# A fixed place in each step for the products that give a row maximum, the difference product last, and five summed tiles in place of four on TensorE

## The chip, the cores and the metric

The kernel runs on one core of a Trainium2 chip. The metric is the device time in microseconds (us) of one execution; lower is better. The numbers of before are the median of three timed runs and one further execution under the hardware profiler, from which all rows of the trace come.

## The reference

Three stages follow each other. Only the first is touched by the change: attention over 2 batches of 8 heads, with 1152 keys of 64 dimensions, and queries that are averaged in twos, so that 576 are left.

```python
q_pool = q.reshape(B, H, S // factor, factor, D).mean(axis=3)
scores = scale * np.matmul(q_pool, k.transpose(0, 1, 3, 2))
scores = scores - np.max(scores, axis=-1, keepdims=True)
attn = np.exp(scores)
attn = attn / (np.sum(attn, axis=-1, keepdims=True) + 1e-09)
return np.matmul(attn, v).astype(np.float32)
```

Its output, 1152 rows of 512, goes through a mixture of experts (8 experts, one per row) and then a dense block with the weights `w_in` and `w_out`.

## The kernel before

The attention works on 8 pairs of heads, p = 0 to 7. A pair has 9 steps, t = 0 to 8, one for each 128 keys. The engines' orders are written out by hand: what the Python loop emits first stands first in the queue of its engine, and each engine works its queue strictly in that order.

**A step** of pair p does three things on TensorE. `scores` makes the transposed scores of 128 keys against all 576 queries of both heads (8 matrix products, L287 to L296), and ScalarE turns them into exponentials, the tile `Pt[p, t]`. `pv` multiplies the exponentials of the step before with the values (L304). And a few products for the row maxima of the next pair, p + 1, are put between.

**The maxima.** The query rows of a pair are cut into 9 units, four of 128 queries for each head and one mixed one. For each unit the 1152 keys are handled in three chunks of 384. Chunk c = 0 is reduced by VectorE (L103). Chunk c = 1 isn't the keys but their difference, `KD` (tile `kx`, made by GpSimd: keys 384 to 767 minus keys 768 to 1151); ScalarE takes the positive part of the product into the buffer `wd` (tile name `wd<-mx` at L91). Chunk c = 2 is added to that and reduced by VectorE (L240). So 27 products per pair, each into one of three PSUM banks called `mx`, which are taken in turn. The same three banks serve `sum_log` (step 2, L344, emptied by ScalarE into `sm`), `sum_tr` (step 3, L351, emptied by `sum_rec` on VectorE in step 4), the output's transposes (L401, steps 5 and 6) and `max_rows` (step 8, L268), which turns the finished maxima into rows for the next pair's scores.

**The denominators.** The exponentials of all keys must be summed. VectorE adds tiles into `St` (`add_tile`, one addition of 128 x 1152), and `psums` sums a tile over its keys with a matrix of ones, on TensorE (L324).

**The end of a pair.** In step 0 of the following pair the last `pv` and `psums` come, and `post_evac` empties the accumulators: ScalarE copies them (`wd<-pv`, `sm<-pv`), then VectorE adds into `sm` (`sm<-pv,sm`). The accumulators are one set, so the first `pv` of the new pair, in step 1, waits for this addition.

**Decoding.** Between all this, a packed weight matrix for the last stage is decoded in 23 blocks. A block is loaded by SyncE into one of two buffers `wraw`; ScalarE takes the absolute value of one half (`dm<-wraw`), GpSimd clamps it, and VectorE does two halves of bit work: part 0 reads `wraw` (`ds<-wraw` twice), part 1 writes the weights (`dm<-dm`, `wd<-dm,ds`). A load waits until part 0 of the block two before is done, since that frees its buffer. In pairs 0 to 6 four or five such halves are done in a pair; pair 7 has no maxima to prepare and does 15 of them (`DEC_L`).

**The order in a step** is spelt by a string: `0` is `scores`, `m` a place for one waiting task and one product, `r` `max_rows`, `p` `pv` with `psums`, `s` and `t` the two sum pieces. Tasks that find no place are emitted at the end of the step.

Of the kernel before, what the change touches and what calls it, by code (L numbers as in the profile page):

```python
# [29 lines left out]
NPAIR = B * H // 2  # L30
KT = S // P
# [53 lines left out]
def kernel(ctx, tc, cst, qt, kt, v, wgo, w1, w2, wio, out):  # L85
# [71 lines left out]
    Pt, pvt = {}, {}  # L157
# [84 lines left out]
    def ahead(units):  # L242
        n = len(units)
        seq_ = [(units[0], 0), (units[0], 1)]
        for i in range(n):
            if i + 1 < n:
                seq_ += [(units[i + 1], 1)]
            seq_ += [(units[i], 2)]
            if i + 1 < n:
                seq_ += [(units[i + 1], 0)]  # L250
        return [(*u, c) for u, c in seq_]

    chunks = ahead([(h, j) for h in range(2) for j in range(4)] + [(0, 4)])

    mfin = {}

# [43 lines left out]
    def pv(p, t, f):  # L300
        if t == 0 and f == 0:
            pvt[p] = pvp.tile([P, 2, 512], F32, name="pv")
        for h in range(2):
            mm(pvt[p][64 * h:64 * h + 64, f, :HQ], lhsT=vt[p][:, t, h, :], rhs=Pt[p, t][:, h, f * HQ:(f + 1) * HQ], start=t == 0, stop=t == KT - 1, skip_group_check=True)  # L304


    adds = {2: True, 3: False, 5: True, 6: False, 8: True}
    whole = {3: (0,), 6: (0,), 8: (0, 1)}
    St = {}

    def add_tile(p, t, new):
# [4 lines left out]
    def psums(p, t):  # L316


        for src in [(St[p], Pt[p, t])[i] for i in whole.get(t, ())]:
            for f in range(2):  # L320
                for h in range(2):
                    for a in range(2):
                        q_, t0 = 64 * h + 32 * a, 256 * a + 160 * f
                        mm(pvt[p][q_:q_ + 32, f, HQ:HQ + 160], lhsT=e2[:, h], rhs=src[:, h, t0:t0 + 160], start=False, stop=src is Pt.get((p, KT - 1)), skip_group_check=True)  # L324
# [13 lines left out]
    def sum_log(p):  # L338

        b, hp = divmod(p, 4)  # L340
        ps = mxp.tile([P, 512], F32, name="mx")
        for a in range(2):
            qs_ = slice(256 * a, 256 * a + 320)
            mm(ps[32 * a:32 * a + 32, :320], lhsT=wbd[:, hp], rhs=xut[p][:, qs_], start=True, stop=True)  # L344
        act(sm[:64, 64 * b:64 * b + 320], ps[:64, :320])

    def sum_tr(p):
        ps = mxp.tile([P, 512], F32, name="mx")
        slt[p] = ps[:, :384].rearrange("p (w c) -> p w c", w=3)
        for w in range(3):  # L350
            T.transpose(slt[p][:, w], sm[:, w * P:(w + 1) * P], ident)  # L351
# [215 lines left out]

    for g in range(-9, 9 * NPAIR):
        p, t = divmod(g, 9)
        if t == 0:  # L570
            todo = list(chunks) if p + 1 < NPAIR else []
        tasks = list(sched.get(g, ()))
        if p >= 0 and t in adds:
            tasks += [lambda: None] * (2 - len(tasks))
            tasks.insert(2, lambda p=p, t=t: add_tile(p, t, adds[t]))
        if p >= 0:
            n = DEC_L[t] if p == NPAIR - 1 else (t in (0, 1, 2, 8)) + (p % 2 and t == 3)
            tasks += [lambda: (raw_ahead(ap, DEC_A), decode_step(ap, DEC_A))] * n
            if t in ABS_T or p == NPAIR - 1:
                tasks.append(lambda: (raw_ahead(ap, DEC_A), decode_abs(ap)))  # L580

        slot = [0]

        def mxc(todo=todo):
            if tasks:
                tasks.pop(0)()
            if todo:
                max_chunk(p + 1, *todo.pop(0))
            slot[0] += 1

        prev = divmod(g - 1, 9)
        seq = "0mmrpsmmt" if p == NPAIR - 1 or t in (2, 3, 4, 8) else "0mmrpsmt"
        if g < 0:
            seq = "mmmm"
        assert not (t == 8 and todo), (p, len(todo))
        for ch in seq:
            if ch == "0":
                if p >= 0:
                    scores(p, t)
            elif ch == "m":  # L600
                mxc()
            elif ch == "s":
                if p > 0 and t == T_S:
                    sum_log(p - 1)
            elif ch == "t":
                if p > 0 and t == T_T:
                    sum_tr(p - 1)
            elif ch == "e":
                mxc([])
            elif ch == "r":  # L610
                if t == 8 and 0 <= p < NPAIR - 1:
                    max_rows(p + 1)
            elif ch in "pfg" and prev[0] >= 0:
                if ch in "pf":
                    pv(*prev, 0)
                if ch in "pg":
                    pv(*prev, 1)
                    psums(*prev)
                    if prev[1] == KT - 1:
                        post_evac(prev[0])  # L620
        for f in tasks:
            f()
        if p > 0 and t in (T_X - 1, T_X):
            x_tr(p - 1, t - T_X + 1)
        if g == -1:
            warm(6)
        if g == -1:
            max_rows(0)
            warm(2)
# [766 lines left out]
```

## Time and profile before

| | |
|---|---|
| median of 3 runs | 691.23 us (690.6 to 692.02) |
| profiled execution, its own time | 691.73 us |
| its span, first to last instruction | 689.9 us |
| outside the span | 1.83 us |
| mean granted TensorE clock | 0.981 of full speed |
| TensorE matmul busy | 638.6 us (93%) |
| VectorE busy | 510.7 us (74%) |
| ScalarE busy | 398.4 us (58%) |
| attention, steps of pairs 0 to 7 | from 22 us to 292 us of the span |

Read it like this: the busy share of TensorE comes from matrix products that are pipelined, with modelled ends, so it overstates the work; what counts is the distance from one start to the next. The start of a pair is where the first `scores` product (L287) of its step 0 starts: 22.26, 54.53, 88.96, 122.36, 156.48, 190.57, 225.30 and 257.73 us.

### The profile page before, as it was taken

What the parts mean: (1) busy time and instruction counts of PE and PEld (TensorE: products, weight loads), DVE (VectorE), ACT (ScalarE), POOL (GpSimd) and SP (SyncE); (2) the same over time, 40 slices, a digit from 0 to 9 for tenths busy, and PEclk for the clock granted to TensorE, in tenths of its full rate; (3) what the DMA queues carried; (4) which work ended last, traced back from release to release, by engine and by line L of the source; (5) the groups of instructions that cost most, each with busy time, mean ns of one, the idle gap of its engine ahead of it and who ended that gap; (6) DMA issues with size and microseconds to landing.
All of it is one profiled execution on the core that took longest, in us unless ns stands there. A gap on an engine that the chain in (4) does not pass through costs nothing. (4 is left out here: it accounts for less than half of the span.)

```text
span 689.9 us, 11179 instructions
## 1 busy us (share of the span) xinstructions
PE 638.6 (93%) x4079; PEld 495.4 (72%) x4079; DVE 510.7 (74%) x1028; ACT 398.4 (58%) x825; POOL 210.4 (31%) x178
## 2 busy tenths in 40 slices
PE   4899999999999998859979999988899999999997
PEld 3666666666666665529866977757788999999995
DVE  5777878787878888756653988314999977897775
ACT  7877676767676765425244538324665554555543
POOL 7531504142223114334121524202222232233322
PEclk9999999999999999979989999999999999999999
DMA  7673645453524204249479878561000020001001
GB/s 267 210 214 86 173 116 145 130 150 118 132 82 137 96 1 142 81 129 351 169 294 320 311 249 324 209 246 47 0 1 1 0 93 2 0 1 47 1 0 47
DMA packets 26641, 88.32 MB, mean 128 GB/s; under 512 B 2886, under 2 KB 7631, under 8 KB 22482
## 3 DMA queue, kind: packets, MB, share of 16 engines
q1 hardware_dynamic: 21264, 73.23, 30.2%
q0 software_dynamic: 3568, 8.79, 5.7%
q10 hardware_dynamic: 1746, 5.51, 2.3%
q8 instruction: 34, 0.56, 0.3%
q14 instruction: 29, 0.24, 0.1%
HBM read 79.65 MB, written 8.39 MB: 128 GB/s over the span
## 5 line engine op out<-in xcount | busy, mean ns | idle before, releaser
L91 ACT ACTIVATE pt<-sc 128x320 f32<-128x320 f32 (+1 forms) x216 | 94.6, 489 | 20.5 <-PE sc L289 18.0
L100 POOL TENSOR_SCALAR u<-u 128x384 f32<-128x384 f32 x48 | 59.8, 1247 | 152.5 <-ACT u L91 120.4
L304 PE MATMUL pv<-pt,vt 128*64 128x288 f32 x576 | 86.5, 423 | 0.6 <-DVE sm L94 0.5
L100 POOL TENSOR_SCALAR dm<-dm 128x512 f32<-128x512 f32 x23 | 51.6, 2242 | 83.5 <-ACT dm L91 76.1
L865 PE MATMUL zps<-yh,wh 128*128 128x384 f32 x188 | 64.4, 343 | 1.7 <-DVE n L97 1.7
L867 PE MATMUL zps<-yl,wh 128*128 128x384 f32 x188 | 63.5, 338 | 0.0
L866 PE MATMUL zps<-yh,wd 128*128 128x384 f32 x180 | 61.1, 340 | 0.0
L1305 PE MATMUL ops<-wh,gl 128*128 128x512 f32 x144 | 57.8, 404 | 3.0 <-DVE gl L94 2.4
L304 PEld LDWEIGHTS pv<-pt,vt 128*64 128x64 f32 x576 | 35.4, 137 | 32.0 <-issue 15.1
L1305 PE MATMUL ops<-wh,gh 128*128 128x512 f32 x144 | 56.8, 394 | 0.2 <-ACT gh L91 0.2
L1305 PE MATMUL ops<-wd,gh 128*128 128x512 f32 x135 | 53.1, 393 | 0.0
L226 PE MATMUL mx<-at,qs 128*128 128x384 f32 x120 | 40.5, 381 | 11.7 <-ACT at L91 6.7
L103 DVE TENSOR_REDUCE Mp<-mx 128x1 f32<-128x384 f32 x72 | 39.7, 551 | 8.1 <-PE mx L226 7.1
L91 ACT ACTIVATE wd<-mx 128x384 f32<-128x384 f32 x63 | 30.9, 493 | 25.4 <-PE mx L226 17.1
L240 DVE CUSTOM_DVE_ANT_0 wd<-mx,wd 128x384 f32<-128x384 f32 x63 | 34.7, 551 | 14.1 <-PE mx L230 7.3
L91 ACT ACTIVATE l<-n,two 128x384 f32<-128x384 f32 x48 | 29.5, 614 | 25.0 <-DVE n L97 25.0
L91 ACT ACTIVATE u<-zps 128x384 f32<-128x384 f32 x48 | 23.2, 483 | 32.8 <-PE zps L867 30.1
L97 DVE SCALAR_TENSOR_TENSOR l<-n,r 128x384 f32<-128x384 f32 x48 | 26.6, 554 | 19.8 <-ACT r L91 19.8
L865 PEld LDWEIGHTS zps<-yh,wh 128*128 128x128 f32 x188 | 35.6, 190 | 3.7 <-ACT r L91 2.0
L226 PEld LDWEIGHTS mx<-at,qs 128*128 128x128 f32 x120 | 22.2, 197 | 21.0 <-ACT at L91 6.9
L1305 PEld LDWEIGHTS ops<-wh,gl 128*128 128x128 f32 x144 | 27.0, 188 | 13.9 <-DVE gl L94 7.0
L91 ACT ACTIVATE gh<-n 128x384 fp32r<-128x384 f32 x48 | 24.8, 517 | 20.7 <-DVE n L97 20.2
(293 smaller groups left out, 1742.2 us busy)
## 6 DMA issues: line engine op xcount, KB each, us to landing
wt<-in_w SPq DMA_DIRECT2D x32, 1024.0 KB, 6.2
wraw<-in_wio SPq DMA_DIRECT2D x23, 512.0 KB, 4.5
kd<-in_kt SPq DMA_DIRECT2D x16, 576.0 KB, 3.8
vt<-in_v SPq DMA_DIRECT2D x8, 576.0 KB, 6.6
wraw<-in_wio ACTq DMA_DIRECT2D x9, 512.0 KB, 6.1
tq<-in_qt SPq DMA_DIRECT2D x12, 288.0 KB, 4.9
tq<-in_qt POOLq DMA_DIRECT2D x12, 288.0 KB, 4.3
pt<-in_qt SPq DMA_DIRECT2D x4, 576.0 KB, 5.8
```

The lines of the kernel that those rows point to most:

```text
L91: A.activation(out=out, in_=in_, func=func, **kw)
L97: V.scalar_tensor_tensor(out=out, in0=a, scalar=s, in1=b, op0=op0, op1=op1)
L100: eng.tensor_scalar(out=out, in0=a, scalar1=s1, scalar2=s2, op0=op0, op1=op1)
L103: V.tensor_reduce(out=out, in_=in_, axis=AX.X, op=op)
L226: mm(ps, lhsT=QS[p, h][:, j * P:(j + 1) * P], rhs=keys(h), start=True, stop=True)
L240: V.tensor_tensor_reduce(out=r_, in0=ps, in1=r_, scale=1.0, scalar=-3.0e38, op0=ALU.add, op1=ALU.max, accum_out=Mp[p % 2][:, h, j, 1:2])
L304: mm(pvt[p][64 * h:64 * h + 64, f, :HQ], lhsT=vt[p][:, t, h, :], rhs=Pt[p, t][:, h, f * HQ:(f + 1) * HQ], start=t == 0, stop=t == KT - 1, ...
L865: mm(out_, lhsT=a, rhs=c, start=first, stop=False)
L866: mm(out_, lhsT=b_, rhs=c, start=False, stop=False)
L867: mm(out_, lhsT=a, rhs=d, start=False, stop=last_)
L1305: mm(opt[b_, j], lhsT=(g_, g_, gl_)[i], rhs=(wo, wl_, wo)[i], start=f == 0 and i == 0, stop=f == NF - 1 and i == 2)
```

## The change

The string is gone, and two tables say which products belong to which step: `EARLY[t]` before `pv`, `LATE_[t]` after it. A unit's products c = 0 and c = 2 now stand before `pv`, and the next unit's c = 1 (the difference) after it, in the same step. In step 2 there are six products, three on either side; the first c = 1 of a pair is made already in step 8 of the pair before. The addition of step 8 is left out; `psums` sums five tiles in place of four: `St`, `St` and `Pt[p, 6]`, `Pt[p, 7]` and `Pt[p, 8]`. The decoding half of step 2 moves to step 3, the additional one of odd pairs from step 3 to step 8. Tasks are emitted before `pv` only with a product or while more than three are waiting (in step 8: all).

```diff
-    chunks = ahead([(h, j) for h in range(2) for j in range(4)] + [(0, 4)])
+    units = [(h, j) for h in range(2) for j in range(4)] + [(0, 4)]
+    chunks = ahead(units)
+    EARLY = [[(0, 0), (0, 2)], [(1, 0), (1, 2)], [(2, 0), (2, 2), (3, 1)]] + [[(i, 0), (i, 2)] for i in range(4, 9)] + [[]]
+    LATE_ = [[(1, 1)], [(2, 1)], [(3, 0), (3, 2), (4, 1)]] + [[(i, 1)] for i in range(5, 9)] + [[], [(0, 1)]]
...
-    adds = {2: True, 3: False, 5: True, 6: False, 8: True}
-    whole = {3: (0,), 6: (0,), 8: (0, 1)}
+    adds = {2: True, 3: False, 5: True, 6: False}
+    whole = {3: lambda p: (St[p],), 6: lambda p: (St[p], Pt[p, 6]), 8: lambda p: (Pt[p, 7], Pt[p, 8])}
...
-        for src in [(St[p], Pt[p, t])[i] for i in whole.get(t, ())]:
+        for src in whole[t](p) if t in whole else ():
...
-            n = DEC_L[t] if p == NPAIR - 1 else (t in (0, 1, 2, 8)) + (p % 2 and t == 3)
+            n = DEC_L[t] if p == NPAIR - 1 else (t in (0, 1, 3, 8)) + (p % 2 and t == 8)
...
-        seq = "0mmrpsmmt" if p == NPAIR - 1 or t in (2, 3, 4, 8) else "0mmrpsmt"
...
+            scores(p, t)
+            while todo or len(tasks) > (0 if t == 8 else 3):
+                mxc()
+            todo = late
+            if t == 8 and p < NPAIR - 1:
+                max_rows(p + 1)
+            if prev[0] >= 0:
+                for f in range(2):
+                    pv(*prev, f)
+                psums(*prev)
+                if prev[1] == KT - 1:
+                    post_evac(prev[0])
+            if p > 0 and t == T_S:
+                sum_log(p - 1)
+            while todo:
+                mxc()
+            if p > 0 and t == T_T:
+                sum_tr(p - 1)
```

TensorE in step 2 of pair 4, from the products before `pv` to the next step's first score product (before, then changed; `kx` is the difference, `at` the keys). Lines of the changed kernel are three higher.

```order
L226 MATMUL mx<-at,qs 128x384 x2
L304 MATMUL pv<-pt,vt 64x288 x4
L344 MATMUL mx<-wd,wbd 32x320 x2
L226 MATMUL mx<-kx,qs 128x384
L226 MATMUL mx<-at,qs 128x384
L287 MATMUL sc<-qs,at 128x320
```

```order
L226 MATMUL mx<-at,qs 128x384 x2
L226 MATMUL mx<-kx,qs 128x384
L307 MATMUL pv<-pt,vt 64x288 x4
L347 MATMUL mx<-wd,wbd 32x320 x2
L226 MATMUL mx<-at,qs 128x384 x2
L226 MATMUL mx<-kx,qs 128x384
L290 MATMUL sc<-qs,at 128x320
```

Three products stand on either side of `pv` and `sum_log` now, where two did; seven `mx` banks are taken in the step in place of five.

VectorE from the end of pair 3 through steps 0 and 1 of pair 4, up to the first work of step 2 (before, then changed; `Bt<-kd,at` is the low part of the keys, `qs<-tq,qs` that of the queries, ISA the operation of L240).

```order
L94 TENSOR_TENSOR st<-pt 128x1152
L100 TENSOR_SCALAR dm<-dm 128x512
L97 SCALAR_TENSOR_TENSOR wd<-dm,ds 128x512
L94 TENSOR_TENSOR Bt_112<-kd,at 64x576
L103 TENSOR_REDUCE Mp_117<-mx 128x1
L94 TENSOR_TENSOR sm<-pv,sm 64x320
L100 TENSOR_SCALAR ds<-wraw 128x512
L97 SCALAR_TENSOR_TENSOR ds<-wraw,ds 128x512
L240 ISA wd,Mp_117<-mx,wd 128x384
```

```order
L94 TENSOR_TENSOR Bt_112<-kd,at 64x576
L103 TENSOR_REDUCE Mp_117<-mx 128x1
L240 ISA wd,Mp_117<-mx,wd 128x384
L240 ISA Mp_117 128x1
L94 TENSOR_TENSOR sm<-pv,sm 64x320
L100 TENSOR_SCALAR ds<-wraw 128x512
L97 SCALAR_TENSOR_TENSOR ds<-wraw,ds 128x512
L103 TENSOR_REDUCE Mp_117<-mx 128x1
```

The addition `st<-pt` has gone from ahead of `sm<-pv,sm`, and unit 0's L240 has moved from behind it to ahead of it.

VectorE at the start of pair 7, from the first half of block 15 to the first addition of pair 7 (before, then changed).

```order
L100 TENSOR_SCALAR ds<-wraw 128x512
L97 SCALAR_TENSOR_TENSOR ds<-wraw,ds 128x512
L100 TENSOR_SCALAR dm<-dm 128x512
L97 SCALAR_TENSOR_TENSOR wd<-dm,ds 128x512
L100 TENSOR_SCALAR ds<-wraw 128x512
L97 SCALAR_TENSOR_TENSOR ds<-wraw,ds 128x512
L94 TENSOR_TENSOR sm<-pv,sm 64x320
L100 TENSOR_SCALAR dm<-dm 128x512
L97 SCALAR_TENSOR_TENSOR wd<-dm,ds 128x512
L100 TENSOR_SCALAR ds<-wraw 128x512
L97 SCALAR_TENSOR_TENSOR ds<-wraw,ds 128x512
L94 TENSOR_TENSOR st<-pt 128x1152
```

```order
L100 TENSOR_SCALAR ds<-wraw 128x512
L97 SCALAR_TENSOR_TENSOR ds<-wraw,ds 128x512
L94 TENSOR_TENSOR sm<-pv,sm 64x320
L100 TENSOR_SCALAR dm<-dm 128x512
L97 SCALAR_TENSOR_TENSOR wd<-dm,ds 128x512
L100 TENSOR_SCALAR ds<-wraw 128x512
L97 SCALAR_TENSOR_TENSOR ds<-wraw,ds 128x512
L100 TENSOR_SCALAR dm<-dm 128x512
L97 SCALAR_TENSOR_TENSOR wd<-dm,ds 128x512
L100 TENSOR_SCALAR ds<-wraw 128x512
L97 SCALAR_TENSOR_TENSOR ds<-wraw,ds 128x512
L94 TENSOR_TENSOR st<-pt 128x1152
```

Part 1 of block 15 and part 0 of block 16 stood ahead of `sm<-pv,sm` and stand behind it now: step 0 of pair 7 has three tasks, and three are left until the end of the step.

## Rows read from the trace of the kernel before

**Rows 1.** The page's first line.

```profile
span 689.9 us, 11179 instructions
```

**Rows 2.** Stretches of pairs: start:end, length, busy us (and instructions) per engine, clock, DMA.

```profile
20.00:54.53 34.53, 30.81 (x216) 21.21 (x214) 27.04 (x55) 28.01 (x61) 14.18 (x10) 1.00 0.68 201
...
88.96:122.36 33.40, 32.45 (x256) 22.01 (x254) 26.90 (x61) 24.36 (x56) 9.75 (x7) 1.00 0.47 129
...
156.48:190.57 34.09, 32.66 (x256) 22.02 (x255) 27.45 (x61) 24.52 (x56) 8.04 (x7) 1.00 0.44 126
190.57:225.30 34.73, 32.76 (x257) 22.09 (x255) 29.04 (x63) 24.93 (x57) 10.12 (x7) 1.00 0.36 109
225.30:257.73 32.43, 32.07 (x257) 22.10 (x256) 26.59 (x62) 22.67 (x52) 5.92 (x4) 1.00 0.15 52
```

**Rows 3.** Timeline of TensorE, pair 4, steps 0 to 4: start, us, instruction, idle before.

```profile
159.22 0.75 PE L324 MATMUL pv<-st,e 128*32 128x160 f32 x16
159.79 0.73 PE L324 MATMUL pv<-pt,e 128*32 128x160 f32 x16
160.44 0.44 PE L226 MATMUL mx<-kx,qs 128*128 128x384 f32 x1
160.72 0.31 PE L287 MATMUL sc<-qs,at 128*128 128x320 f32 x1
...
166.36 0.73 PE L344 MATMUL mx<-wd,wbd 128*32 128x320 f32 x4
167.68 0.44 PE L226 MATMUL mx<-kx,qs 128*128 128x384 f32 x1 [0.59 <-DVE Mp L240]
...
168.43 0.31 PE L287 MATMUL sc<-qs,at 128*128 128x320 f32 x1
...
169.50 0.34 PE L226 MATMUL mx<-at,qs 128*128 128x384 f32 x1
169.68 0.34 PE L226 MATMUL mx<-kx,qs 128*128 128x384 f32 x1
169.95 1.19 PE L304 MATMUL pv<-pt,vt 128*64 128x288 f32 x8
171.07 0.62 PE L226 MATMUL mx<-at,qs 128*128 128x384 f32 x2
...
173.86 0.44 PE L226 MATMUL mx<-kx,qs 128*128 128x384 f32 x1 [0.53 <-DVE Mp L240]
...
176.96 0.32 PE L287 MATMUL sc<-qs,at 128*128 128x320 f32 x1
```

**Rows 4.** Timeline of VectorE in the same pair, steps 0 to 2.

```profile
161.78 0.48 DVE L94 TENSOR_TENSOR sm<-pv,sm 64x320 f32<-64x320 f32 x1 [3.19 <-ACT sm L91]
...
163.49 0.55 DVE L240 CUSTOM_DVE_ANT_0 wd<-mx,wd 128x384 f32<-128x384 f32 x1
...
167.07 0.55 DVE L240 CUSTOM_DVE_ANT_0 wd<-mx,wd 128x384 f32<-128x384 f32 x1
```

**Rows 5.** Timeline of ScalarE in the same pair, step 2.

```profile
167.84 0.42 ACT L91 ACTIVATE sm<-mx 64x320 f32<-64x320 f32 x1
```

**Rows 6.** The tile St: count, shortest, median and longest ns, first and last start.

```profile
L94 DVE TENSOR_TENSOR st<-pt x24: 1339/1348/1359, 33.5 to 287.9; 128x1152 f32<-128x1152 f32 x24
```

**Rows 7.** Pair 7: SyncE, ScalarE and VectorE timelines; the waits of ScalarE, 257 to 293.

```profile
260.55 19.15 SPq L436 DMA_DIRECT2D wraw<-in_wio  x5
...
265.39 0.68 ACT L91 ACTIVATE dm<-wraw 128x512 f32<-128x512 f32 x1 [0.55 <-DMA wraw<-in_wio]
...
259.79 0.69 DVE L97 SCALAR_TENSOR_TENSOR ds<-wraw,ds 128x512 int32<-128x512 int32 x1
262.68 0.48 DVE L94 TENSOR_TENSOR sm<-pv,sm 64x320 f32<-64x320 f32 x1 [2.20 <-PE sc L296]
...
ACT dm L91 <- DMA wraw<-in_wio: 5.7, 4, 3.1
```

**Rows 8.** One us of pair 7, step 6, with the columns of group 2.

```profile
282.00:283.00 1.00, 1.00 (x5) 0.54 (x6) 0.97 (x3) 0.84 (x2) 0.00 (x0) 0.50 0.29 119
```

More of the change, by code (lines that the diff above doesn't have):

```diff
@@ L569 @@
         p, t = divmod(g, 9)
-        if t == 0:
-            todo = list(chunks) if p + 1 < NPAIR else []
+        if t == 0 and p < 0:
+            todo = list(chunks)
+        if p >= 0:
+            todo = [(p + 1, *units[u], c) for u, c in EARLY[t]] if p + 1 < NPAIR else []
+            late = [(p + 1 + (t == 8), *units[u], c) for u, c in LATE_[t]] if p + 1 + (t == 8) < NPAIR else []
+            if g == 0:
+                todo.insert(0, (1, *units[0], 1))
         tasks = list(sched.get(g, ()))
@@ L580, with mxc @@
                 tasks.append(lambda: (raw_ahead(ap, DEC_A), decode_abs(ap)))
-        slot = [0]
-        def mxc(todo=todo):
+        def mxc():
             if tasks:
@@ L587, in mxc @@
             if todo:
-                max_chunk(p + 1, *todo.pop(0))
-            slot[0] += 1
+                c_ = todo.pop(0)
+                max_chunk(*(c_ if p >= 0 else (0, *c_)))
         prev = divmod(g - 1, 9)
-        seq = "0mmrpsmmt" if p == NPAIR - 1 or t in (2, 3, 4, 8) else "0mmrpsmt"
[L593 to L600, printed above, removed]
-                mxc()
[L602 to L620, printed above, removed]
+        if p < 0:
+            for _ in range(4):
+                mxc()
+            assert t < 8 or not todo, todo
+        else:
+            scores(p, t)
[16 more added lines that the diff above has]
+                sum_tr(p - 1)
         for f in tasks:
```

## The prediction

> **What bounds the kernel now.** I read the page first, then the stretches of the eight pairs, then the three engines' timelines of one pair, and last the order in which the change puts the instructions. The span is 689.9 us [rows 1]; with 1.83 us around it the profiled execution took 691.73 us, 0.5 us above the median of the runs shown. Pairs 1 to 5 last, by their starts, 34.43, 33.40, 34.12, 34.09 and 34.73 us, pairs 0 and 6 32.3 (its first scores start at 22.26) and 32.43, all at full granted clock [rows 2]. TensorE is busy for 32 to 33 us of each, VectorE for 27 to 29, ScalarE for 24 to 25. So TensorE bounds the pairs, and what can be won is the time in which it waits.
>
> Where it waits is seen in pair 4. In step 2 the product at 167.68 waits for a free `mx` bank, until VectorE has done the L240 that started at 167.07; in step 4 the product at 173.86 waits in the same way [rows 3, 4]. The reason lies further back. In step 0 VectorE comes to `sm<-pv,sm` and stands for 3.19 us, because the accumulators are summed and copied only then [rows 4]. From 161.78 on it works without a gap and is behind TensorE until step 4. Step 2 ends at 168.43, and steps 3 and 4 take 8.53 us up to 176.96 [rows 3].
>
> **The change part by part.** *Work added to TensorE.* A summed tile more per pair: the second source follows the first after 159.79 - 159.22 = 0.57 us [rows 3]. That is 0.57 us in each of 8 pairs, all on the engine that bounds them.
>
> *Work taken from VectorE.* One addition per pair, 1.35 us [rows 6]. It was the addition of step 8, just ahead of the stand of 3.19 us [rows 4]; where it stood, VectorE now waits longer for the same thing. I count it at nothing. The L240 that moves from behind the stand to ahead of it helps no more: from 163.49 to 167.07 VectorE did six things (that L240, a klo, an L103, a qlo and a half block in two), and the changed order (its rows stand with the diff) has the same six up to the first maximum of step 2, with the L240 now that of unit 1. So the L103 of step 2 starts at about the same 167.07.
>
> *Step 2* (times of pair 4, to be set beside it). `sum_log` is now the fourth bank of the step, and its bank is freed by that L103. It can start at 167.07 + 0.55 + 0.05 = 167.67, where it started at 166.36 [rows 3, 4]. Then (3,0) and (3,2) run, and (4,1) takes the bank that ScalarE empties with its copy of 0.42 us [rows 5]: 0.73 for the sums, 0.42 and two handovers of about 0.05 make 168.9; with 0.28 for the last product (160.72 - 160.44 [rows 3]) the step ends at 169.2, 0.8 us later than before. But three more products of this pair have been made by then, one of them already in step 8 before.
>
> *Steps 3 and 4.* A step's scores take 169.50 - 168.43 = 1.07 us, a product 0.18, `pv` 171.07 - 169.95 = 1.12 [rows 3]. Before, the two steps had two scores (2.14), two `pv` (2.24), eight products (1.44), one summed tile (about 0.65) and about 0.5 of transposes and changes between kinds of work: 7.0, so 1.5 of 8.53 were waits. Now they have six products, and the addition of step 2 is no longer followed by a half block, which moved behind the next addition. I follow the banks: L103 of (3,0) frees one at about 169.8, L240 of (3,2) one at 170.3, `sum_rec` that of `sum_tr` near 174.9, each before TensorE comes to it (at 170.3, 170.5 and 175.6). So 6.65 us in place of 8.53, a gain of 1.9.
>
> *The others.* Steps 0, 1, 5 and 6 hold the same work before and after: nothing. Step 7 has the second source (0.57) and one product with its change of kind less (0.28): +0.3. In step 8 the maxima are ready before `max_rows` asks for them, but the next scores wait for ScalarE, which writes their rows after its exponentials; the extra product hides in that: -0.1. The sum for pair 4 is 0.8 - 1.9 + 0.3 - 0.1 = -0.9 us. The waits of pair 2 are smaller, those of pair 5 larger. I take the new length 33.2 for all five, 166.2 against 170.8: -4.6. Pair 6 had no wait in step 2 and gains 0.4; pair 0 has no `sum_log`, and its step 2 waits for a decoding that stays: I take 0.4. Pairs 0 to 6 together: -5.4. Bounds: nothing, if each wait only moves; -11, if step 2 doesn't wait either (1.1 more in five pairs).
>
> *Pair 7.* It has no maxima, and so 15 halves of decoding; ScalarE waits four times, 5.7 us together, for packed blocks to land, and its next exponentials stand behind [rows 7]. A load goes out when part 0 of the block two before it is done. Part 0 of block 16 ended at 259.79 + 0.69 = 260.48; the load of block 18 went out at 260.55, and ScalarE got on at 265.39 [rows 7]. In the changed order this half stands behind `sm<-pv,sm`, which starts at 262.68 and can't move: TensorE and ScalarE must first finish pair 6. With 0.5 for that addition and two halves of 1.1 to 1.6 the load goes out at about 265.9, 5.4 us later. The landing then takes 3.8 to 4.8 us, so ScalarE waits until about 270, and the exponentials of step 2 and the scores of step 3 behind it come 3.5 us late. Of the following waits, for blocks 19 to 21, which before were waits too, some of it is taken back: block 19's falls away, those of 20 and 21 come again, since their loads hang on part 0 after an addition that needs these exponentials. I take 2.9 us for what is left, and 0.57 for the summed tile, which near the end has no cover: +3.5. Bounds: 0.6, if the delay is taken back wholly; 6.0, if none of it is.
>
> **The sum.** -5.4 + 3.5 = -1.9 against 691.73, so 689.8 for a profiled execution, and 0.5 less for the median of timed runs: about 689.3.
>
> **The clock.** In pair 7 the granted clock was at 0.50, the 1.2 GHz level, in the us from 282.00, after steps in which TensorE stood between products [rows 8]. The longer stand around 268 can make this come earlier or twice. The Trainium skill, page "TensorE: Matmul & The Clock Gate", section "HAM oscillation — how this bites in real kernels", says that gaps in which TensorE idles bring the lower clock back; the trace agrees with that much, by the one us named. If it comes earlier, it falls into steps where ScalarE waits for loads, and costs nothing; if it comes a second time, in steps that TensorE sets, each such step has 1.07 + 1.12 us of work that doubles, so +2.2 us for one step and 4.4 for two.
>
> **The rivals.**
> 1. *The last pair pays little* (the load of block 18 is late, but the pair has slack). For it: ScalarE idles in pair 7 and three of four loads are late anyway. Against: the chain from load to exponentials to addition to the next load is closed. Then -5.4 + 0.6: 686.4.
> 2. *Slower: step 2 becomes a queue.* Seven banks are taken in one step from a ring of three, while VectorE is still behind from its stand. Each of the later three may wait for its own turn of VectorE (an L103 of 0.55, and the addition of 1.35 that stands between), up to 1.9 us more in step 2. Priced at the 1.1 us a pair with which the pairs just gain nothing, 689.3 + 5.4 gives 694.7. It decides from 0.7 us more of waiting per pair: five times that is the way from 689.3 to 692.6, where slower begins. For it: the addition stands between the maxima of (2,2) and of (3,0). Against: these banks are needed only in step 3.
> 3. *No change to be seen*: the pairs gain 4 and the last gives 4 back: 691.
> 4. *The clock falls twice* in pair 7: 691.5 to 693.7.
>
> **How the numbers follow.** Chances: forecast (687.5 to 690.5) 0.42, the first rival 0.18, the second 0.17, the third 0.15, the fourth 0.08. A measurement of this kernel can tell about 0.2%, 1.4 us, from no change, so faster is below 689.85. Three quarters of the forecast and all of the first rival give faster 0.5; the rest of the forecast, the third and a part of the fourth give same 0.28; slower 0.22. The range leaves out the far ends of the first two rivals: 684.5 to 694.5; the forecast's own is 687.5 to 690.5.
>
> **What the profile of the changed kernel would show.** Right: pairs 1 to 5 at about 33.2 us each; in step 2 a wait of about 1.2 us before `sum_log` (L347) for VectorE's L103; no wait over 0.2 us in step 4; VectorE's stand before `sm<-pv,sm` longer than 3.19 us less the L240; in pair 7 a load that goes out 3 us after `sm<-pv,sm` starts, behind it one wait of ScalarE for a block of 4 to 5 us in step 1, and pair 7 about 3.5 us longer. Wrong: pairs of 34 us with the wait in step 2 above 2.5 us (second rival), or a pair 7 that isn't longer (first rival).

## The result, and the profile after

The changed kernel takes 699.11 us (median of 4 runs, 696.95 to 699.54), the kernel before 691.11 beside it: the ratio is 1.0108, with a 95% interval of 1.0085 to 1.0131. It is slower, and the 689.3 us and the range of the prediction missed it. The profiled execution took 699.12 us.

The first lines of its page:

```profile
span 697.3 us, 11410 instructions
...
PE 640.6 (92%) x4207; PEld 499.5 (72%) x4207; DVE 501.4 (72%) x1020; ACT 397.2 (57%) x825; POOL 208.7 (30%) x178
```

VectorE has 9.3 us less to do than before, and the span is 7.4 us longer: what was taken from VectorE did not shorten the time. The stretches of the eight pairs, cut at the first score product of each and for the last at its step 8 (columns as in [rows 2]):

```profile
20.00:55.59 35.59, 31.55 (x232) 21.89 (x231) 26.75 (x54) 27.66 (x61) 15.11 (x10) 1.00 0.60 193
55.59:89.44 33.85, 32.73 (x271) 22.53 (x271) 26.15 (x59) 24.43 (x56) 9.92 (x7) 1.00 0.48 130
89.44:125.50 36.06, 34.13 (x272) 23.55 (x271) 25.89 (x59) 24.86 (x57) 10.93 (x8) 0.95 0.48 133
125.50:158.88 33.38, 32.43 (x271) 22.42 (x271) 27.04 (x61) 24.32 (x56) 9.10 (x7) 1.00 0.44 120
158.88:192.85 33.97, 32.71 (x272) 22.46 (x272) 27.03 (x59) 24.45 (x56) 8.20 (x7) 1.00 0.49 142
192.85:226.96 34.11, 32.85 (x272) 22.47 (x272) 28.54 (x61) 24.45 (x56) 7.29 (x6) 1.00 0.36 111
226.96:260.42 33.46, 32.39 (x272) 22.31 (x271) 24.64 (x59) 22.68 (x53) 7.95 (x5) 1.00 0.19 65
260.42:292.20 31.78, 26.76 (x223) 16.76 (x221) 23.99 (x44) 15.86 (x35) 12.95 (x7) 0.95 0.30 102
```

The first scores of pair 0 start at 22.21, so pairs 0 to 6 take 238.21 us, where they took 257.73 - 22.26 = 235.47 [rows 2]: 2.7 longer, where 5.4 shorter was forecast. The kernel before, profiled once more (r2_before_again below), took 236.23 for the same pairs, its pair 0 alone 33.04 in place of 32.27, so some 0.8 of the 2.7 is scatter between executions. Pairs 1, 3, 4 and 5 won 0.58, 0.74, 0.12 and 0.62; pairs 0, 2 and 6 lost 1.1, 2.7 and 1.0. Pair 7 up to its step 8 went from 30.01 to 31.78. Here too one execution of before is a narrow base: in r2 the same pair took 28.66, with the clock's fall (0.50, from 277.8 us on) earlier in it:

```profile
258.45:287.11 28.66, 25.75 (x207) 16.21 (x205) 23.93 (x44) 15.67 (x35) 12.44 (x7) 0.94 0.39 122
```

The rest of the 7.4 us, 2.9, lies behind the attention: from the first matrix product of the counts to the end 394.1 us, 391.2 before.

Pair 4, on whose rows the prediction was worked out, came nearly as drawn (TensorE's timeline, to be set beside [rows 3]):

```profile
169.97 0.73 PE L347 MATMUL mx<-wd,wbd 128*32 128x320 f32 x4 [0.87 <-DVE Mp L103]
...
174.22 0.44 PE L226 MATMUL mx<-kx,qs 128*128 128x384 f32 x1
...
178.14 0.44 PE L226 MATMUL mx<-kx,qs 128*128 128x384 f32 x1
```

Step 2 took 5.56 us (5.5 forecast) with the wait before `sum_log` for VectorE's L103; steps 3 and 4 took 6.84 without a wait (6.65 forecast). But step 6 is 0.58 longer than before. Pairs 2 and 6 show something that pair 4 doesn't have. Pair 2, steps 1 and 2, on TensorE, GpSimd and ScalarE:

```profile
101.70 0.44 PE L226 MATMUL mx<-at,qs 128*128 128x384 f32 x1 [0.19 <-ACT wd L91]
103.00 0.44 PE L226 MATMUL mx<-kx,qs 128*128 128x384 f32 x1 [0.85 <-POOL kx L94]
...
99.67 2.00 POOL L100 TENSOR_SCALAR dm<-dm 128x512 f32<-128x512 f32 x1 [5.22 <-ACT dm L91]
101.65 1.30 POOL L94 TENSOR_TENSOR kx<-kd 128x384 fp32r<-128x384 f32 x1
...
98.73 0.26 ACT L91 ACTIVATE QM<-qs 128x64 fp32r<-128x64 f32 x1 [0.89 <-DVE qs L97]
98.90 0.68 ACT L91 ACTIVATE dm<-wraw 128x512 f32<-128x512 f32 x1
```

The reader is to see a chain over three engines. VectorE begins the same block in the same place in both kernels (`ds<-wraw` at 98.73, before at 98.48). But ScalarE takes the absolute value of a block ahead of that where it can, and before it had done so in pair 1:

```profile
78.86 0.67 ACT L91 ACTIVATE dm<-wraw 128x512 f32<-128x512 f32 x1
```

In the changed order one half less has been decoded by then, and ScalarE comes to this block only at 98.90, when VectorE needs it. Its `dm` makes GpSimd clamp for 2.00 us, and the key difference `kx` of the second head, which before was done at 94.05, far ahead of any clamping, now stands behind. Its product waits 0.85 us. In pair 6 the same rows stand at 236.25, 238.22 and 239.58, with 0.84 us. What came behind it in pair 2 is in the granted clock (windows of 2 and 1.5 us):

```profile
101.50:103.50 2.00, 0.95 (x5) 0.69 (x5) 1.53 (x4) 0.49 (x3) 1.45 (x2) 1.00 0.93 284
103.50:105.00 1.50, 1.50 (x8) 1.50 (x7) 0.00 (x0) 0.92 (x3) 0.00 (x0) 0.50 0.97 353
```

TensorE was busy for 0.95 of the 2 us up to 103.50, and then had 0.50, the 1.2 GHz level; step 3 took 4.68 us, where pair 4 took 3.16.

Pair 1 waits in step 2 for another engine (TensorE, ScalarE, VectorE):

```profile
65.65 0.44 PE L226 MATMUL mx<-kx,qs 128*128 128x384 f32 x1 [1.02 <-ACT wd L91]
...
64.96 0.26 ACT L91 ACTIVATE QM<-qs 128x64 fp32r<-128x64 f32 x1 [1.46 <-DVE qs L97]
65.12 0.47 ACT L91 ACTIVATE wd<-mx 128x384 f32<-128x384 f32 x1
...
64.17 0.76 DVE L97 SCALAR_TENSOR_TENSOR qs<-tq,qs 64x576 fp32r<-64x576 f32 x1
```

The positive part `wd<-mx` of the product that now comes late in step 1 is queued behind the copy `QM`, which waits for VectorE's query part `qs`, which stands behind the maxima and the half block. Its `mx` bank comes free 1.02 us late.

Pair 7 shows the late load that was forecast (SyncE, VectorE and ScalarE, beside [rows 7]):

```profile
268.29 3.12 SPq L439 DMA_DIRECT2D wraw<-in_wio  x2
...
265.37 0.48 DVE L94 TENSOR_TENSOR sm<-pv,sm 64x320 f32<-64x320 f32 x1 [7.76 <-PE sc L299]
...
271.96 0.67 ACT L91 ACTIVATE dm<-wraw 128x512 f32<-128x512 f32 x1 [2.94 <-DMA wraw<-in_wio]
```

The load goes out 2.9 us after the addition starts (3 forecast), and ScalarE waits for it, 2.94 us where 4 to 5 were forecast.

### The profile page after: what moved, and what is told of

Same layout as the page of the kernel before. It is cut to its first block, busy times and chain, and to the rows that moved or that the text cites. A ratio compares the mean times of both kernels' runs of the same rounds, so it can differ in the third digit from the quotient of the medians.

```text
span 697.3 us, 11410 instructions
## 1 busy us (share of the span) xinstructions
PE 640.6 (92%) x4207; PEld 499.5 (72%) x4207; DVE 501.4 (72%) x1020; ACT 397.2 (57%) x825; POOL 208.7 (30%) x178
## 3 DMA queue, kind: packets, MB, share of 16 engines
HBM read 79.65 MB, written 8.39 MB: 126 GB/s over the span
## 5 line engine op out<-in xcount | busy, mean ns | idle before, releaser
L91 ACT ACTIVATE pt<-sc 128x320 f32<-128x320 f32 (+1 forms) x216 | 93.2, 489 | 13.4 <-PE sc L292 11.4
L100 POOL TENSOR_SCALAR dm<-dm 128x512 f32<-128x512 f32 x23 | 48.1, 2094 | 101.1 <-ACT dm L91 101.1
L103 DVE TENSOR_REDUCE Mp<-mx 128x1 f32<-128x384 f32 x72 | 39.8, 552 | 32.6 <-PE mx L226 31.5
L226 PE MATMUL mx<-at,qs 128*128 128x384 f32 x120 | 36.1, 368 | 10.3 <-DVE qs L97 7.9
L867 PEld LDWEIGHTS zps<-yl,wh 128*128 128x128 f32 x188 | 35.6, 189 | 0.0
L240 DVE CUSTOM_DVE_ANT_0 wd<-mx,wd 128x384 f32<-128x384 f32 x63 | 34.4, 546 | 1.2 <-PE mx L226 1.1
```

Of the source, the lines that this page charges most:

```text
L91: A.activation(out=out, in_=in_, func=func, **kw)
L100: eng.tensor_scalar(out=out, in0=a, scalar1=s1, scalar2=s2, op0=op0, op1=op1)
L103: V.tensor_reduce(out=out, in_=in_, axis=AX.X, op=op)
L226: mm(ps, lhsT=QS[p, h][:, j * P:(j + 1) * P], rhs=keys(h), start=True, stop=True)
L240: V.tensor_tensor_reduce(out=r_, in0=ps, in1=r_, scale=1.0, scalar=-3.0e38, op0=ALU.add, op1=ALU.max, accum_out=Mp[p % 2][:, h, j, 1:2])
L867: mm(out_, lhsT=a, rhs=d, start=False, stop=last_)
```

## The experiments

All ratios are to the kernel before, run on the same chip (691.11 us beside the changed kernel, 692.16 to 692.73 beside the others). "Pairs 0 to 6" is the distance from the first scores of pair 0 to those of pair 7, "pair 7" from there to its step 8, in the profiled execution.

| | median us | ratio [95%] | pairs 0 to 6 | pair 7 |
|---|---|---|---|---|
| before | 691.1 to 692.7 | 1 | 235.5 | 30.0 |
| changed | 699.11 | 1.0108 [1.0085, 1.0131] | 238.2 | 31.8 |
| e1_sums | 697.35 | 1.0062 [1.0042, 1.0082] | 242.7 | 29.4 |
| e2_tables | 694.35 | 1.0021 [0.9998, 1.0045] | 233.6 | 31.5 |
| e3_decode_back | 699.41 | 1.0087 [1.0053, 1.0121] | 238.7 | 31.9 |
| e4_pair7_tasks | 698.16 | 1.0076 [1.0048, 1.0103] | 238.3 | 29.1 |
| e5_two_mends | 695.24 | 1.0028 [1.0009, 1.0048] | 237.2 | 30.6 |
| e6_mends_4tiles | 688.02 | 0.9935 [0.9912, 0.9957] | 231.2 | 30.0 |
| e7_tables_pair7 | 689.39 | 0.9943 [0.9919, 0.9967] | 233.6 | 28.5 |
| e8_mends_qm | 685.09 | 0.9897 [0.9864, 0.9931] | 228.7 | 28.4 |
| e9_mends_5tiles | 691.08 | 0.9976 [0.9957, 0.9995] | 232.4 | 29.4 |
| e10_mends_left_out | 687.27 | 0.9924 [0.9899, 0.9949] | 228.6 | 28.5 |
| e11_mends_decode | 690.93 | 0.9969 [0.9950, 0.9988] | 233.9 | 30.1 |
| e12_before_left_out | 692.76 | 0.9994 [0.9974, 1.0013] | 237.2 | 28.6 |
| r1_changed_again | 702.62 | 1.0142 [1.0080, 1.0205] | 238.1 | 31.9 |
| r2_before_again | 691.16 (one run) | | 236.2 | 28.7 |
| r3_left_out_again | 685.64 | 0.9898 [0.9871, 0.9924] | 228.7 | 28.5 |

**The parts of the change, one by one.** *e1_sums*: the kernel before with the five summed tiles alone (`psums` reads `whole` as in the change).

```diff
-    adds = {2: True, 3: False, 5: True, 6: False, 8: True}
-    whole = {3: (0,), 6: (0,), 8: (0, 1)}
+    adds = {2: True, 3: False, 5: True, 6: False}
+    whole = {3: lambda p: (St[p],), 6: lambda p: (St[p], Pt[p, 6]), 8: lambda p: (Pt[p, 7], Pt[p, 8])}
```

> The kernel before with the five summed tiles alone: the addition of step 8 is gone, the order of the products and the decoding are those of before. Theory of the parts (each part has its own price on TensorE): the second source of step 7 costs 0.57 us in each of 8 pairs and VectorE's addition gives nothing back, so about +4 us. Rival (VectorE's relief counts): steps 0 to 2 of the next pair are earlier by up to 1.3 us, and the time is the same or lower.

Slower by 0.62%. Pairs 1 to 4 and 6 are 0.52 to 0.55 us longer each than in [rows 2], and a fall of the clock in pair 5 makes 36.85 of 34.73. Pair 0 is 2.5 longer, with a fall in it too, from 33.5 us on: the profiled execution took 703.70 us, 6.35 more than the median.

*e2_tables*: the order of the change (tables and tasks), without its sums and its decoding (against the changed kernel; `whole` is that of before too).

```diff
-    adds = {2: True, 3: False, 5: True, 6: False}
+    adds = {2: True, 3: False, 5: True, 6: False, 8: True}
...
-            n = DEC_L[t] if p == NPAIR - 1 else (t in (0, 1, 3, 8)) + (p % 2 and t == 8)
+            n = DEC_L[t] if p == NPAIR - 1 else (t in (0, 1, 2, 8)) + (p % 2 and t == 3)
```

> The changed order of products, with the four summed tiles and the decoding places of before. Theory of the parts: pairs 1 to 5 fall to about 32.7 us each and pairs 0 to 6 gain 5 us or more; pair 7 still has its late load, about +1.5 us; so 4 us below before. Rival (the six products of step 2 are the loss): pairs stay at 34 us or more and the time is that of the changed kernel less 3 us, about 696.

The order alone shortens pairs 0 to 6 by 1.9 us and lengthens pair 7 by 1.5 (against r2 2.6 and 2.9). Neither forecast of the time came: 694.35 can't be told from before, where 4 us less, or about 696, was expected.

*e3_decode_back*: the changed kernel with the decoding places of before (the second line pair above alone).

> The changed kernel with the decoding places of before. Theory (in pairs 2 and 6 the moved half pulls a clamping of GpSimd ahead of the key difference, and TensorE waits for that difference in step 2): these waits of 1.1 us go, with the lower clock that follows in pair 2, but VectorE has a half more in step 2 of every pair; pairs 2 and 6 shorter by 1 to 2.5 us, the others longer by up to 0.5. Rival (the wait for the difference is not from the decoding): pairs 2 and 6 stay at 36.1 and 33.5 us.

Pairs 2 and 6 lose their wait for `kx` and get 2.15 and 0.77 us shorter; pairs 0, 1 and 3 get 0.6, 1.3 (with a fall of the clock) and 1.1 us longer, pairs 4 and 5 0.2. The moved decoding is harm in two pairs and help in the others; only in pair 1 the 1.3 is no more than what a fall costs (r1 below).

**The last pair.** *e4_pair7_tasks*: the changed kernel, in whose pair 7 two tasks of a step stand ahead of `pv` and all others after it (the expectation has the two sides exchanged).

```diff
-            while todo or len(tasks) > (0 if t == 8 else 3):
+            keep = 0 if t == 8 else 3 if p < NPAIR - 1 else max(len(tasks) - 2, 0)
+            while todo or len(tasks) > keep:
```

> The changed kernel with all but two of a step's tasks of pair 7 kept ahead of the products with the values, as before, so that the half of block 16 that frees its buffer stands ahead of the addition into sm. Theory (the late load costs pair 7 1.8 us): pair 7 is shorter by 1.2 to 2 us, the rest the same, about 697.5. Rival (pair 7 is longer for the summed tile and the clock alone): no change, 699.

Pairs 0 to 6 are the same, pair 7 is 2.7 us shorter, more than the 1.2 to 2 expected. The load goes out 5.4 us before the addition (SyncE and VectorE):

```profile
260.29 8.98 SPq L439 DMA_DIRECT2D wraw<-in_wio  x2
...
265.73 0.48 DVE L94 TENSOR_TENSOR sm<-pv,sm 64x320 f32<-64x320 f32 x1 [5.51 <-PE sc L299]
```

So the late load costs 2.7 us, with the effect of the clock: there is no fall in this pair 7, and one from 274.2 us on in that of the changed kernel.

*e7_tables_pair7*: e2_tables with the same edit.

> e2_tables (the changed order of the products of the maxima, with the four tiles and the decoding places of before) with the last pair's tasks as in e4_pair7_tasks. Theory that the late load is all that e2_tables lost in the last pair: pair 7 from 31.5 to about 29 us until step 8 starts, the pairs 0 to 6 as they were (233.6), the time 2 to 2.7 us below e2_tables, about 691.7, just below before. Rival, the last pair's gain is used up by a wait in the stages behind it (counts, experts), as the time of e4_pair7_tasks fell by less than half of its 2.7 us: the time stays at 693.5 to 694.5.

Pair 7 takes 28.5 in place of 31.5, part of which may be the clock's (it falls at 275.8, and at 278.7 in e2), and the time falls by 5 us at the medians (on two chips, whose kernel before differs by 0.2). This is already faster than before.

**The waits in pairs 2, 6 and 1.** *e5_two_mends*: e4_pair7_tasks with the second head's `kx` a step earlier.

```diff
-... (khi(p, h, 0), qlo(p, h)))
+... (khi(p, h, 0), qlo(p, h), kdiff(p, h) if h else None))
...
-... (khi(p, h, 1), kdiff(p, h)))
+... (khi(p, h, 1), None if h else kdiff(p, h)))
```

> The changed kernel with two places mended: in the last pair two tasks of a step instead of all but three stand ahead of the products of the values (as in e4_pair7_tasks), and the key differences of the second head (kx) are issued one step earlier, so that GpSimd does them ahead of the clamping of a decoded block. Theory of two defects: what the change lost is the late load (2.7 us, pair 7 to the start of step 8 near 29.1 us) and the wait of 0.85 us for kx in step 2 of pairs 2 and 6 with the fall of the clock behind it in pair 2; the lengths of pairs 2 and 6 come to about 33.5 and 32.6 us instead of 36.06 and 33.46, the sum of pairs 0 to 6 to about 234.8 instead of 238.2, and the time to about 693. Rival, the clock's falls are only moved: pairs 2 and 6 lose their wait, but TensorE falls to the lower clock in another pair, the sum of pairs 0 to 6 stays at 237 to 239 and the time at 696 to 698, as in e3_decode_back.

In pair 2 `kx` is ready at 98.3, and its product waits no longer (GpSimd, TensorE):

```profile
97.34 0.99 POOL L94 TENSOR_TENSOR kx<-kd 128x384 fp32r<-128x384 f32 x1
102.71 2.00 POOL L100 TENSOR_SCALAR dm<-dm 128x512 f32<-128x512 f32 x1 [4.37 <-ACT dm L91]
...
105.15 0.41 PE L226 MATMUL mx<-kx,qs 128*128 128x384 f32 x1
```

Pair 2 takes 33.72 us in place of 36.08 (e4), pair 6 32.53 in place of 33.47. Both theories have a share: the waits are gone, and the clock now falls in pair 0 (a granted mean of 0.90 over 23.0 to 58.5), which took 35.57 in place of 33.37 in this execution (699.40 us, the slowest of twelve). The time fell by 2.9 us at the medians, to 695.24, between the two forecasts.

*e8_mends_qm*: e6_mends_4tiles (below) with the copy `QM` of the second head a step later, in the task of step 2 in which `kx` was.

```diff
+        if h == 0 or p == 0:
+            qmix(p, h)
...
-... (khi(p, h, 1), None if h else kdiff(p, h)))
+... (khi(p, h, 1), qmix(p, h) if h else kdiff(p, h)))
```

> e6_mends_4tiles with one more move: the copy of the second head's query part into the shared tile (QM) is issued one step later, behind the key parts of step 2, so that ScalarE's relu of the step before no longer stands behind a copy that waits for VectorE. Theory that TensorE's wait of 1.02 us for that relu in step 2 of pair 1 is lost time: pair 1 is about 1 us shorter than in e6_mends_4tiles and the others are the same, the time about 1 us less. Rival, ScalarE's order only shifts the wait to the exponentials of step 2: pair 1 and the time stay within 0.3 us.

ScalarE in pair 1:

```profile
62.34 0.51 ACT L91 ACTIVATE wd<-mx 128x384 f32<-128x384 f32 x1
...
64.40 0.31 ACT L91 ACTIVATE QM<-qs 128x64 fp32r<-128x64 f32 x1
```

`wd<-mx` doesn't wait for the copy any more, and pair 1 is 0.97 us shorter (32.36 for 33.33). Pairs 3, 4 and 5, expected to stay, are 0.4 shorter each, in step 2 (5.16 us, 5.54 to 5.56 in e6): before `sum_log` TensorE waited there 0.88 us in e6, put down to VectorE's L103, and now up to 0.49, put down to `wd<-mx`. In pair 4:

```profile
163.22 0.73 PE L351 MATMUL mx<-wd,wbd 128*32 128x320 f32 x4 [0.47 <-ACT wd L91]
```

By which path the copy had delayed `sum_log` can't be told from these rows. This is the fastest kernel: 685.09 us, 1.0% below before.

**The fifth tile.** *e6_mends_4tiles*: e5_two_mends with the sums of before (the first line of e2's diff, and `whole` of before).

> e5_two_mends with the sums of before: four tiles to the ones matrix in a pair, and a third addition in step 8 on VectorE. Theory that the fifth tile is paid in full: e1_sums lost about 0.55 us in a pair by it, so every pair is about 0.55 us shorter than in e5_two_mends, some 4.4 us over the eight pairs, and the time near 689, below before. Rival, in the changed order step 8 waits for the addition on VectorE again (the products of the summed tile are late), or TensorE waits elsewhere for the time that it saves: the time is within 0.2% of e5_two_mends.

Pairs 1 to 7 are 0.51 to 0.57 us shorter than in e5, as the theory says; pair 0 is 2.7 shorter, since the clock's fall in it is gone.

*e9_mends_5tiles*: e8_mends_qm with the sums of the change (e1's lines).

> e8_mends_qm with the five summed tiles of the change, and without the addition of step 8: the changed kernel with all three mends. Theory that the fifth tile is paid in full on TensorE: every pair is 0.50 to 0.58 us longer than in e8_mends_qm, as e5_two_mends stands to e6_mends_4tiles, 4.4 us over eight pairs, so the time at 689.5 or a little above. Rival, most of the 7.2 us between e5_two_mends and e6_mends_4tiles was the clock's fall in pair 0 and not the tile: the time is within 2 us of 685.1.

The theory holds (691.08 us, far outside the rival's 2 us of 685.1); the pairs are set side by side with e10's below.

*e10_mends_left_out*: e8_mends_qm with neither the addition nor the tile.

```diff
+    adds = {2: True, 3: False, 5: True, 6: False}
+    whole = {3: lambda p: (St[p],), 6: lambda p: (St[p],), 8: lambda p: (Pt[p, 7], Pt[p, 8])}
```

> e8_mends_qm without the addition of step 8 and with four summed tiles: the exponentials of one tile of a pair (step 6) are left out of the denominators, so neither engine pays for them. Theory that VectorE's relief is worth nothing: the time is that of e8_mends_qm within 1.4 us (683.7 to 686.5), and all that e9_mends_5tiles loses is the products of the tile. Rival, the addition holds up step 8 or the end of a pair: the pairs are at least 0.3 us shorter each and the time is 682.7 or below.

*e12_before_left_out*: the kernel before with these two lines.

> The kernel before without its addition of step 8 and with four summed tiles; the exponentials of step 6 are left out of the denominators. Theory that VectorE's relief is worth nothing in the order of before either: the time is within 1.4 us of the kernel before, and the 4.8 us of e1_sums are the products of the fifth tile with what they trigger. Rival, the relief is worth something that e1_sums hid: 1.5 to 4 us faster than before, and a tile costs that much more than 0.57 us in a pair.

Pair 3, cut at its first scores, of e8 (addition, four tiles), then e10 (neither), then e9 (no addition, five tiles):

```profile
120.07:152.52 32.45, 31.91 (x255) 21.97 (x255) 27.24 (x62) 24.22 (x56) 9.04 (x7) 1.00 0.47 125
```

```profile
120.12:152.58 32.46, 31.91 (x255) 22.01 (x255) 27.02 (x61) 24.20 (x56) 9.04 (x7) 1.00 0.47 125
```

```profile
122.18:155.17 32.99, 32.44 (x271) 22.52 (x271) 27.02 (x61) 24.21 (x56) 9.09 (x7) 1.00 0.45 121
```

Without the addition pairs 0 to 6 are as long as with it, to 0.05 us; a tile more (e9 against e10) costs 0.52 to 0.56 in each of them and 0.86 in pair 7, 4.6 us together. The time of e10 itself, 687.27, missed its theory's 683.7 to 686.5; what it has more than e8 lies behind the attention (395.0 us for 392.2), and the same kernel again came to 685.64. e12 agrees for the order of before: no difference that its interval can tell, and its pairs 1 to 4 and 6 are those of before to 0.03 us (pair 5, with a fall of the clock from 210.1 us on, is 1.6 longer). The addition was free in the pairs, and the tile that replaced it is paid in full.

**The decoding.** *e11_mends_decode*: e8_mends_qm with the decoding places of before.

> e8_mends_qm with the decoding places of before (a half in step 2 in place of step 3, the additional one of odd pairs in step 3 in place of step 8). Theory that the moved decoding did harm by kx alone, which is mended: the time is that of e8_mends_qm within 1.4 us. Rival, a half in step 2 stands in front of the maxima there: pairs 0, 1 and 3 lose 0.6 to 1.3 us, as e3_decode_back did against the changed kernel, and the time is 687.5 to 689.

The rival holds, and more than it said: pairs 0 to 6 lose 5.2 us, from 0.2 in pair 2 to 1.4 and 1.5 in pairs 1 and 3. Pair 3, VectorE and TensorE:

```profile
133.87 1.35 DVE L94 TENSOR_TENSOR st<-pt 128x1152 f32<-128x1152 f32 x1
135.13 0.42 DVE L100 TENSOR_SCALAR dm<-dm 128x512 int32<-128x512 int32 x1
135.59 0.69 DVE L97 SCALAR_TENSOR_TENSOR wd<-dm,ds 128x512 int32<-128x512 int32 x1
136.20 0.55 DVE L103 TENSOR_REDUCE Mp<-mx 128x1 f32<-128x384 f32 x1
...
136.81 0.45 PE L230 MATMUL mx<-at,qs 128*128 128x384 f32 x1 [0.65 <-DVE Mp L103]
```

Behind the addition of step 2 the half block stands between VectorE and the maximum for whose bank step 3 waits. Moved, it stands behind the next addition, where no bank is due. With the waits mended the move is therefore the most valuable part of the change.

**The stages behind the attention.** Three kernels again: *r1_changed_again*, *r2_before_again*, *r3_left_out_again* (e10).

> The changed kernel once more. In its first profile the stages behind the attention, whose code the change doesn't touch, took 394.1 us from the first matrix product of the counts to the end of the span, against 391.2 in the kernel before. Theory that this is scatter between executions: the stretch differs from 394.1 by 1 us or more in this profile, the steps of the pairs 1 to 6 are the same to 0.1 us. Rival, it belongs to the program (the moment at which the stage starts against its loads): 394.1 within 0.5 us again.

> The kernel before once more, for the same question. Scatter: the stretch behind the attention comes out 1 us or more away from 391.2. Property of the program: 391.2 within 0.5 us.

> e10_mends_left_out once more, whose pairs are as long as those of e8_mends_qm to 0.05 us, and which still took 2.2 us more at the median: its stretch behind the attention took 395.0 us against 392.2. Scatter between executions: another value, 1 us or more away, and a median nearer to 685.1. Property of the program: 395.0 within 0.5 us and 687.3 again.

The changed kernel came out at 702.62 us beside 692.5, a ratio of 1.0142 [1.0080, 1.0205]; e10 at 685.64, 0.9898 [0.9871, 0.9924]. The stretch behind took 394.6, 391.2 and 392.6 us. The first two are the same to 0.5, the third is 2.4 away from its 395.0. In the changed kernel it is split otherwise (first the part up to the products of the last stage, then the rest; the first two rows are of the first profile, the others of r1):

```profile
303.20:466.80 163.60, 151.63 (x953) 120.80 (x952) 96.03 (x202) 72.77 (x147) 49.43 (x43) 0.96 0.75 273
466.80:697.30 230.50, 217.24 (x1083) 192.11 (x1083) 177.75 (x314) 118.50 (x224) 62.49 (x51) 0.98 0.05 19
```

```profile
303.30:470.30 167.00, 153.97 (x953) 122.85 (x952) 96.26 (x202) 72.94 (x147) 49.81 (x43) 0.94 0.76 268
470.30:697.90 227.60, 215.52 (x1083) 190.60 (x1083) 177.86 (x314) 118.83 (x224) 63.37 (x51) 0.99 0.05 19
```

Once the 3 us were lost in the second part, once in the first. They aren't one wait with a place, and as e10 shows, the stretch scatters by more than 2 us in one program. The traces narrow it down: from the first product into `zps`, where the last stage's main products begin, to the last product all 17 profiled executions take 213.99 to 214.09 us. In the first profile of the changed kernel 1.5 us more lie behind that (5.61 us from the last product to the end, 4.09 before), and 2.6 more just ahead of it (10.94 us from `yb<-tri` to `zps`, 8.39 before), where the clock fell at 468.7; 1.1 is won earlier. The first profile of e10 has a fall in the same place (10.04 us), its repetition has none (8.39). In r1 the 3.4 us are spread over four parts, with a fall at 315.5 that before doesn't have. Why the changed kernel lost about 3 us in both profiles stays open.

r1 also shows what a fall of the clock is worth. Its pairs 1 and 2:

```profile
55.68:90.92 35.24, 34.20 (x272) 22.97 (x271) 26.17 (x59) 24.45 (x56) 9.93 (x7) 0.95 0.47 126
90.92:125.45 34.53, 32.61 (x271) 22.50 (x271) 25.88 (x59) 24.80 (x57) 11.41 (x8) 1.00 0.54 137
```

Here the clock fell in pair 1, from 66.3 us on, behind its wait of 1.01 us (the first profile has a wait of 1.02 there and no fall), and not in pair 2, whose wait of 0.83 us is there as before. Pair 1 is 1.4 us longer than in the first profile, pair 2 1.5 shorter. So a fall costs some 1.5 us in a pair that TensorE bounds, and which of two waits brings it changes from one execution to the next. Where TensorE waits anyway a fall can cost nothing: in e4 one stands at 26.1 us, in pair 0, whose steps 0 and 1 are 1.5 us longer and whose step 2, with its waits, is 1.5 shorter (33.37 us for 33.38).

## Why the prediction was wrong

- **The step that failed is "I take the new length 33.2 for all five" with the 0.4 each for pairs 0 and 6.** Pair 4's walk was taken for all pairs. It was nearly right where it was made: steps 2 to 4 of pairs 1, 3, 4 and 5 gained 0.71, 0.87, 0.84 and 1.39 us, against 1.1 forecast. In pair 4 it was partly luck: step 2 met its 5.5 us with a wait of 0.87 for the L103 in place of 1.2, and 0.4 of its 5.56 were the `QM` copy, which the prediction didn't have (e8). The term of -5.4 came out +2.7 (+2.0 against r2), a miss of 8.1. By pairs it is 8.3, since five pairs of 33.2 are 166.0 and not the 166.2 of the prediction.
- **The miss by pairs.** Pair 2 makes 2.9 of it and pair 6 1.4: the `kx` behind a clamping, with the clock behind that in pair 2 (shown by e5, which gave back 2.4 and 0.9). Pairs 1, 3, 4 and 5 make 2.5: the `QM` copy in front of the positive part (shown by e8, which gave 0.97 in pair 1 and 0.4 in three others), and in pairs 4 and 5 step 6, longer by 0.58 and 0.62 (see the last section). Pair 0 makes 1.5: its step 0, 1.5 us longer, holds one product more and waits 1.08 us for ScalarE's `at`, and its step 2 waits 1.25 for `wd<-mx`. Pair 0 was read from the trace and not tried, and r2, whose step 2 waits 1.22 for `wd<-mx` too, takes 0.8 of the 1.5 away. With the three mends and the five tiles (e9) pairs 1 to 5 take 166.8 us together: the forecast length was reached once the waits that the prediction didn't see were gone.
- **The moved decoding was counted as VectorE's work only.** In pair 4 the half behind the next addition was in the gain of steps 3 and 4, rightly: e11 prices it at 5.2 us over the pairs. That the move also changes in which step ScalarE and GpSimd begin a block wasn't followed, and there the harm was (2.1 us in pair 2 and 0.8 in pair 6 come back when it is undone, e3).
- **The tile, 0.57 us in each pair:** right, 0.52 to 0.56. **VectorE's addition counted at nothing:** right, in both orders (e10, e12).
- **Pair 7, +3.5:** the mechanism and its size were right. The late load is worth 2.7 (2.9 taken) and the tile 0.86 (0.57 taken). The pair came out only 1.8 longer than in the execution that the prediction was read from, since the clock's fall, which had cost something in its steps 6 and 7 [rows 8], came earlier. Against r2, whose fall came earlier as well, it is 3.1 longer, and 3.3 in r1. e8 and e6 differ in this: their falls stand at

```profile
270.00:273.40 3.40, 3.40 (x15) 1.78 (x14) 1.95 (x3) 1.30 (x3) 0.95 (x2) 0.51 0.38 135
```

```profile
278.50:281.90 3.40, 3.40 (x16) 2.14 (x13) 3.26 (x8) 1.58 (x4) 1.31 (x1) 0.53 0.03 12
```

and their pairs 7, of the same code, take 28.4 and 30.0 us. The early fall, among ScalarE's waits for loads, costs nothing that can be seen, as the prediction said of it; the late one costs 1.6.
- **The second rival**, a queue in step 2, was on the right side (694.7), and its condition, 0.7 us more of waiting in a pair, is met by single waits in step 2 of pairs 1, 2 and 6 (1.02, 0.85 and 0.84 us). But its mechanism was another: VectorE's turns. The waits that came were ended by ScalarE and GpSimd, whose queues the prediction didn't follow.
- **The stages behind the attention** were counted at nothing, and took 2.9 us more, of which 2.6 came with a fall of the clock and 1.5 behind the last product, about 1.1 being won back. What brought these, and the 3.4 us of r1, is open.

The page "TensorE: Matmul & The Clock Gate" of the Trainium skill, section "HAM oscillation — how this bites in real kernels", lets the lower clock come back after gaps in which TensorE idles. The trace agrees, by the wait of 0.85 us in pair 2 and the 0.50 behind it, and by that of 1.01 us in pair 1 of r1; the same wait of 0.83 us in pair 2 of r1 brought none.

## What to carry to other kernels

Walk through every period of a pipelined loop, not a typical one, when a second schedule with another period (here 4 or 5 halves a pair) is moved against it: the harm was in two pairs of seven. Follow each moved task on all engines it feeds, and ask on each queue what it now stands ahead of. An operation moved from an engine that has slack to the engine that bounds is paid in full; and a slower change may hold a faster one: here the order with three small mends and without the fifth tile is 1.0% faster than before.

## What the hardware showed beside it

VectorE's subtraction `Bt<-kd,at` (64 x 576) takes 0.74 or 0.75 us in 22 of its 26 places in the changed kernel, 0.96 and 0.98 in two, and 2.23 in two, in pairs 4 and 5, where GpSimd does its subtraction `kx` at the same time (VectorE, then GpSimd):

```profile
180.35 2.23 DVE L94 TENSOR_TENSOR Bt<-kd,at 64x576 fp32r<-64x576 f32 x1
...
184.26 0.67 DVE L94 TENSOR_TENSOR wd<-mx,rc 128x512 f32<-128x512 f32 x1
...
180.66 1.31 POOL L94 TENSOR_TENSOR kx<-kd 128x384 fp32r<-128x384 f32 x1
```

It ends 0.61 us after `kx`, of the 0.74 that it takes alone. The delay of 1.5 us reaches the output's product at 184.26, and TensorE's step 6 behind it, the 0.58 us that pair 4 lost there. It comes with the moved decoding: with the places of before (e2, e3, e7, e11) pairs 4 and 5 take 3.18 and 3.20 us for step 6 as before, and pair 3, where the subtraction takes 2.25 to 2.27 there, 3.76 to 3.78. The Trainium skill, page "SBUF — State Buffer", section "Who interferes with whom", says that a VectorE instruction with two SBUF inputs contends with a GpSimd instruction that reads SBUF, that the shared ports are an exclusive lock, and that the order of issue decides who blocks. The trace agrees with the contention by the 2.23 us; by the recorded starts VectorE was first here, by 0.31 us, and still waited. In pair 1 it is the other way round: `kx`, recorded at 78.33, 0.33 us ahead of VectorE's `st<-pt`, took 2.54 us, where it takes 0.99 to 1.00 alone. So the recorded starts don't tell who holds the ports. GpSimd was also issuing a load (`tq<-in_qt`, 180.01 to 180.91) when the subtraction began; at 144.99, 0.25 us into such an issue without `kx`, it took 0.74, so the issue alone isn't the cause.
